# The first chain's spectral product summed on VectorE, with halves exchanged by ScalarE

## The chip, the cores and the metric

The kernel runs on one core of one Trainium2 chip. The metric is the device time of one execution in microseconds (us), and the figure compared is the median of several runs. TensorE (PE in the profile) multiplies matrices, VectorE (DVE) and ScalarE (ACT) work element by element and may read the matmul results in PSUM, GpSimd (POOL) fills tables, and SyncE (SP) issues all the DMAs.

## The reference

Two branches work on the same input `A_u` (2048 positions, 448 channels) and are mixed by a gate:

```python
dt = jnp.exp(log_dt)
A = -jnp.exp(log_A_real) + 1j * A_imag
C = (C_real + 1j * C_imag) * dt[:, None]
P = jnp.exp((A * dt[:, None])[:, :, None] * pos[None, None, :])
K = 2.0 * jnp.einsum("dn,dnl->dl", C, P).real        # 448 kernels, 2048 long, from 256 states each
Kf = jnp.fft.rfft(K, 2 * L)
Uf = jnp.fft.rfft(u_t, 2 * L)
a = irfft(Uf * Kf)[:, :, :L] + u * D_skip            # causal convolution of every channel
b = (sigmoid(x @ w_gate) * (x @ w_up)) @ w_down      # 448 -> 1792 -> 448
g = sigmoid((x * gate_w).sum(-1, keepdims=True))
out = g * a + (1 - g) * b
```

Everything is float32. The change concerns the product `Uf * Kf` and the first step of the inverse transform.

## The kernel before

**Stages.** A prologue makes the parameters. Then `kgen` generates the 448 convolution kernels in 28 chunks of 16 channels, with work on all five engines. The GLU branch (`glu_up`, `glu_down`) is a long stream of matmuls (`gu` for the two projections up, `dn` for the one down) with few demands on other engines. The convolution is a class `Chain`. It makes the spectrum of `u` for both halves of the channels, and later runs once for each half, 224 channels each. The chain of half 0 (called chain 0 here) has its data in the tile `fx_fu`, its PSUM in `fps_fups` (two buffers) and the spectrum of `u` in `uax_fk`. The chain of half 1 (chain 1) has `fx_fk`, `fps_fkps` (three buffers) and `ua_fk`. Both chains run late, side by side, with GLU matmuls between them.

**One chain.** The long transform is split into two short ones with a transpose between. `stage1` multiplies by the first table (L812) and ScalarE copies the results back (L815). `transpose` goes through DRAM for chain 0 (four DMAs to `shf`, four back) and over VectorE for chain 1 (eight `STREAM_TRANSPOSE`, L826). Then `product` walks over eight blocks of four rows. In each block `spectrum_four` (L845) makes two PSUM tiles `p[0]` and `p[1]`, of 128 partitions by 448, by four matmuls on 64 by 64 quadrants of the array; `product_four` multiplies and transforms back (L889); ScalarE copies the two results to `x` (L762). At the end the data are transposed back, and `back` multiplies by the last table (L926), and VectorE scales by the gate and adds to the GLU's part (L930).

**The product.** A spectrum is complex. In a PSUM tile the real parts stand in one group of 32 partitions and the imaginary parts in the next. DRAM holds the spectrum of `u` in a form in which the real part (c = 0) and the imaginary part (c = 1) are each repeated over both groups, so `ua` has the shape 128 x 2 x 2 x 448: partition, c, z, columns. VectorE multiplies both c at once by the same `p[z]` (L879, 896 columns). The sum of the complex product is then left to TensorE. The constant `m_sb` holds the inverse matrix and a second one, turned by a quarter (multiplied by i); the matmuls for c = 0 use the first and those for c = 1 the second, and both accumulate in the same PSUM tile `y[z]`. That makes eight matmuls for a block.

**The order of the work** is not found by a run-time scheduler. The kernel records every operation with its engine, cost, operands and priority (`op`), and the table `PLACE` gives for every kind (engine, tile, priority) the places that its operations take in their engine's queue. `Plan.order` merges the five queues by a small clock model, and the instructions are issued in that order. Each engine works its queue strictly in order. Semaphores are then set between the engines by what each instruction reads and writes.

Tags name the buffers of a pool. `SX` and `SK` give their numbers for the two chains: `ft` tables, `ua` tiles of `u`'s spectrum, `fps` PSUM tiles.

Of the kernel before, what the change touches and what calls it, by code (L numbers as in the profile page):

```python
# [28 lines left out]
    ('Act', 'aci', 10): (15, 36,),  # L29
    ('Act', 'aci', 19): (64, 87,),  # L30
    ('Act', 'acr', 10): (13, 34, 43,),
    ('Act', 'acr', 19): (60, 85, 94,),
# [26 lines left out]
    ('Act', 'dots', 1): (27,),  # L59
    ('Act', 'dots', 2): (50,),  # L60
    ('Act', 'dots', 16): (80, 82,),
# [18 lines left out]
    ('Act', 'idn', 10): (14,),  # L80
    ('Act', 'junk', 10): (28, 61,),
    ('Act', 'junk', 19): (73, 83, 117,),
# [12 lines left out]
    ('Act', 'pos_sb', 10): (75, 53,),  # L95
# [607 lines left out]
def gated_mix(ctx: ExitStack, tc, u, ut, aim, cre, cim, ldt, dskip, gw,  # L703
# [60 lines left out]
    class Chain:  # L764
# [111 lines left out]
        def product_four(self, ua, b):  # L876
# [15 lines left out]
            for z in range(2):  # L892
                evac(lambda r=2 * b + z: self.pair(r), y[z], [(x, 2 * b + z)], prio)
# [685 lines left out]
```

## Time and profile before

| | |
|---|---|
| median of 3 runs | 691.63 us (690.64 to 692.07) |
| the profiled execution's own time | 690.16 us |
| its span, from first to last instruction | 688.4 us |
| instructions | 16283 |
| DMA | 123.84 MB, 180 GB/s on average |
| mean granted TensorE clock | 0.999 |

The profile is one execution. Its span is 1.76 us shorter than the time of the same execution, for what lies before the first and behind the last instruction, and that time lies 1.47 us under the median of the runs. A group row gives line, engine, operation, `out<-in` with tile names, the shape, the count, and then busy time, mean ns of one, and the engine's idle time just before with what ended it. A timeline row begins with its start and its length, and `x8` at its end merges eight instructions. In a table of windows each engine has its busy time and, in brackets, its number of instructions. A float32 matmul appears as two records.

### The profile page before, as it was taken

What the parts mean: (1) busy time and instruction counts of PE and PEld (TensorE: products, weight loads), DVE (VectorE), ACT (ScalarE), POOL (GpSimd) and SP (SyncE); (2) the same over time, 40 slices, a digit from 0 to 9 for tenths busy, and PEclk for the clock granted to TensorE, in tenths of its full rate; (3) what the DMA queues carried; (4) which work ended last, traced back from release to release, by engine and by line L of the source; (5) the groups of instructions that cost most, each with busy time, mean ns of one, the idle gap of its engine ahead of it and who ended that gap; (6) DMA issues with size and microseconds to landing.
All of it is one profiled execution on the core that took longest, in us unless ns stands there. A gap on an engine that the chain in (4) does not pass through costs nothing.

```text
span 688.4 us, 16283 instructions
## 1 busy us (share of the span) xinstructions
PE 673.8 (98%) x6588; PEld 483.1 (70%) x6588; DVE 602.0 (87%) x699; ACT 510.0 (74%) x928; POOL 274.9 (40%) x280
## 2 busy tenths in 40 slices
PE   9999999999999999999899999999999999999996
PEld 8776667877886687775556676788888766556873
DVE  5999999999999999989999789999973489577976
ACT  5677699899999999999999999999941352233110
POOL 0315268865447656675663845667000000000000
PEclk9999999999999999999999999999999999999999
DMA  9769342656896787737966974457948973979866
GB/s 252 180 177 246 87 108 70 153 138 237 186 182 157 177 215 178 225 112 177 193 171 144 233 199 90 140 168 184 180 100 202 271 235 124 312 246 241 166 179 165
DMA packets 97474, 123.84 MB, mean 180 GB/s; under 512 B 31096, under 2 KB 80568, under 8 KB 96376
## 3 DMA queue, kind: packets, MB, share of 16 engines
q1 hardware_dynamic: 97400, 122.81, 69.8%
q8 instruction: 52, 0.85, 0.5%
q14 instruction: 22, 0.18, 0.1%
HBM read 79.20 MB, written 43.58 MB: 178 GB/s over the span
## 4 chain that ended last, share of the span: by engine, by line
PE 73%; ACT 10%; DVE 8%; DMA 5%; issue 2%; SPq 1%; ACTq 0%; DVEq 0%
PE gu_gps L1414 9%; PE gu_gps L1415 8%; PE gu_gps L1416 8%; PE kp_egp L1281 6%; PE dn_gps L1433 5%; PE dn_gps L1435 4%; PE tp_egp L1232 4%; PE dn_gps L1436 4%; PE dn_gps L1437 4%; PE tp_egp L1223 4%; PE fps_fups L812 3%; PE gu_gps L1418 3%; PE gu_gps L1419 3%; PE fps_fups L845 2%; PE fps_fups L889 2%
## 5 line engine op out<-in xcount | busy, mean ns | idle before, releaser
L1414 PE MATMUL gu_gps<-xs_glu,wh_glu 128*128 128x512 f32 x336 | 144.5, 430 | 1.4 <-DVE hl_glu L1400 0.9
L1416 PE MATMUL gu_gps<-xs_glu,wl_glu 128*128 128x512 f32 x336 | 131.8, 392 | 0.0
L1415 PE MATMUL gu_gps<-xs_glu,wh_glu 128*128 128x512 f32 x336 | 131.7, 392 | 0.0
L1269 DVE TENSOR_TENSOR cs_eg<-cs_eg,es_eg 128x2048 f32<-128x2048 f32 x56 | 129.2, 2307 | 1.4
L1252 DVE TENSOR_TENSOR es_eg<-tb_eg 128x1024 f32<-128x1024 f32 x112 | 110.5, 1003 | 3.0 <-POOL tb_eg L1216 0.9
L1213 POOL TENSOR_TENSOR tb_eg<-tb_eg 128x96 f32<-128x96 f32 (+2 forms) x84 | 107.5, 1284 | 5.9
L1216 POOL TENSOR_TENSOR tb_eg<-tb_eg,bs_eg 128x32 f32<-128x32 f32 x84 | 83.9, 1001 | 5.8
L1414 PEld LDWEIGHTS gu_gps<-xs_glu,wh_glu 128*128 128x128 f32 x336 | 63.2, 188 | 30.2 <-issue 13.0
L1398 ACT ACTIVATE sg_glu<-gu_gps 128x512 f32<-128x512 f32 x56 | 33.7, 603 | 58.3 <-PE gu_gps L1419 58.3
L1266 DVE TENSOR_TENSOR cs_eg<-cs_eg,es_eg 128x1024 f32<-128x1024 f32 x56 | 70.5, 1260 | 7.2 <-ACT cs_eg L1245 6.0
L1229 ACT ACTIVATE nn_eg<-cs_eg 128x512 fp32r<-128x512 f32 x112 | 71.7, 640 | 4.5 <-PE tp_egp L1232 2.9
L1415 PEld LDWEIGHTS gu_gps<-xs_glu,wh_glu 128*128 128x128 f32 x336 | 63.3, 188 | 15.4 <-issue 4.8
L1416 PEld LDWEIGHTS gu_gps<-xs_glu,wl_glu 128*128 128x128 f32 x336 | 63.1, 188 | 14.5
L1452 DVE SCALAR_TENSOR_TENSOR ob_glu<-dn_gps,og,ob_glu 128x448 f32<-128x448 f32 x72 | 48.7, 676 | 25.1 <-PE dn_gps L1437 24.1
L1234 ACT ACTIVATE cs_eg<-tp_egp 128x512 f32<-128x512 f32 x112 | 66.5, 605 | 4.1 <-PE tp_egp L1232 3.6
L1227 ACT ACTIVATE cs_eg<-tp_egp 128x512 f32<-128x512 f32 x112 | 67.9, 607 | 1.6 <-PE kp_egp L1281 0.6
L1235 ACT ACTIVATE cs_eg<-tp_egp 128x512 f32<-128x512 f32 x112 | 67.3, 606 | 1.6 <-PE tp_egp L1232 1.4
L1245 ACT ACTIVATE cs_eg<-cs_eg,half_pi 128x1024 f32<-128x1024 f32 x56 | 65.2, 1165 | 0.4
L1281 PEld LDWEIGHTS kp_egp<-cs_eg 128*32 128x32 f32 x3584 | 51.5, 110 | 11.7 <-issue 6.3
L1281 PE MATMUL kp_egp<-cs_eg 128*32 128x64 f32 x3584 | 56.3, 220 | 0.5 <-issue 0.4
L1203 POOL MEMSET tb_eg<- 128x96 f32 x28 | 7.8, 285 | 116.4 <-DVE es_eg L1252 105.5
L1232 PE MATMUL tp_egp<-nn_eg,idn 128*128 128x512 f32 x112 | 49.7, 444 | 3.9 <-ACT nn_eg L1229 3.4
(161 smaller groups left out, 1326.2 us busy)
## 6 DMA issues: line engine op xcount, KB each, us to landing
shf<-fx_fu SPq DMA_DIRECT2D x16, 896.0 KB
fx_fu<-shf SPq DMA_DIRECT2D x16, 896.0 KB
us<-fx_fu SPq DMA_DIRECT2D x16, 896.0 KB
xr_glu<-in_w_dram SPq DMA_DIRECT2D x46, 256.0 KB
uax_fk<-us SPq DMA_DIRECT2D x16, 448.0 KB
ua_fk<-us SPq DMA_DIRECT2D x16, 448.0 KB
xr_glu<-in_w_dram SPq DMA_DIRECT2D x17, 224.0 KB
gt_pre<-in_u_dram SPq DMA_DIRECT2D x8, 448.0 KB
```

The source lines that it names most:

```text
L1213: pool(96 * m, lambda n=n, m=m: G.tensor_mul(g3(n + 1, m), g3(1, m), g3(n, 1).to_broadcast([128, 32, 3, m])))
L1216: pool(32, lambda e=e: G.tensor_mul(t(e + 1), t(e), b(3)))
L1227: op("Act", c_act(512, True), lambda: S.activation(cs[:, 1, ds, 32:96], block(tp), AF.Copy, bias=MAGIC), [tp], [(cs, ("s", i))], prio)
L1229: op("Act", c_act(512), lambda: S.activation(block(nn), cs[:, 1, ds, 32:96], AF.Copy, scale=-1.0, bias=MAGIC), [(cs, ("s", i))], [nn], prio)
L1232: op("PE", c_mm(532), lambda: T.matmul(tp.real, idn.real, nn.real, start=False, stop=True, skip_group_check=True), [nn, idn], [tp], prio)
L1252: V.tensor_mul(o.rearrange("p d (i k) -> p d i k", k=ny), x.unsqueeze(3).to_broadcast([128, 16, nx, ny]), y.unsqueeze(2).to_broadcast([128 ...
L1266: op("DVE", c_dve(1024), lambda: V.tensor_mul(cs[:, :, :, 0:32], cs[:, ::-1, :, 63:31:-1], es[:, :, 0:32].unsqueeze(1).to_broadcast([128, ...
L1269: op("DVE", c_dve(2048), lambda: V.tensor_mul(cs[:, :, :, 32:96], cs[:, :, :, 32:96], es[:, :, 32:96].unsqueeze(1).to_broadcast([128, 2, 1 ...
L1281: T.matmul(kp[32 * j:32 * j + 32, q], cs[:, z, 4 * j + q, 64:96], cs[:, z, 4 * j + q, 0:64], start=cs is parts[0] and z == 0 and q == 0, s ...
L1414: T.matmul(p.real, wh[:, k, cs], x[:, k], start=(k == 0), stop=False)
L1415: T.matmul(p.real, wh[:, k, cs], x[:, 4 + k], start=False, stop=False)
L1416: T.matmul(p.real, wl[:, k, cs], x[:, k], start=False, stop=False)
```

## The change

For half 0 alone (`SWAP = (0,)`), the two terms of the complex product are summed ahead of the inverse matmul. The real part of `u`'s spectrum is multiplied by `p[z]` as before, in place and for 448 columns instead of 896. For the imaginary part, ScalarE copies `p[z]` into a new tile `sw` in four pieces of 32 partitions; each piece is read from the neighbouring group, and the pieces that become real parts change their sign. VectorE multiplies `sw` by the imaginary part and adds the result to the first product. The inverse then needs the plain matrix only: four matmuls a block instead of eight. Half 1 is as before. `PLACE` is a new table throughout, since the new operations need places and the others were moved with them.

```diff
-SX = {'ft': 1, 'ua': 2, 'fps': 2}
-SK = {'ft': 2, 'ua': 2, 'fps': 3}
+SX = {'ft': 1, 'ua': 2, 'fps': 2, 'sw': 2}
+SK = {'ft': 2, 'ua': 2, 'fps': 3, 'sw': 2}
+SWAP = (0,)
+PIECE = 540.0
 ...
         def product_four(self, ua, b):
             x, prio, p = self.x, self.prio, self.spectrum_four(b)
+            if self.h in SWAP:
+                self.product_swapped(ua, b, p)
+                return
 ...
+        def product_swapped(self, ua, b, p):
+            prio = self.prio
+            for z in range(2):
+                sw = self.tile("sw", (128, D))
+
+                def turn(z=z, sw=sw):
+                    for a in range(4):
+                        S.activation(sw[32 * a:32 * a + 32], p[z][32 * (a ^ 1):32 * (a ^ 1) + 32, :D], AF.Copy,
+                                     scale=1.0 if a % 2 else -1.0)
+                op("Act", 4 * PIECE, turn, [p[z]], [sw], prio)
+                op("DVE", c_dve(D, False), lambda z=z: V.tensor_mul(ua[:, 0, z], ua[:, 0, z], p[z][:, :D]),
+                   [p[z]], [(ua, (0, z))], prio)
+                op("DVE", c_dve(D), lambda z=z, sw=sw: V.tensor_mul(sw.real, ua[:, 1, z], sw.real),
+                   [(ua, (1, z))], [sw], prio)
+                op("DVE", c_dve(D), lambda z=z, sw=sw: V.tensor_add(ua[:, 0, z], ua[:, 0, z], sw.real),
+                   [sw], [(ua, (0, z))], prio)
+            y = [self.psum(1), self.psum(1)]
+
+            def f():
+                for z in range(2):
+                    for i in range(2):
+                        rows, to = slice(64 * i, 64 * i + 64), slice(64 * (i ^ z), 64 * (i ^ z) + 64)
+                        T.matmul(y[z][to, :D], m_sb[rows, 64:128], ua[rows, 0, z], start=True, stop=True)
+            op("PE", c_mm64(D), f, [(ua, (0, 0)), (ua, (0, 1)), m_sb], y, prio)
+            for z in range(2):
+                evac(lambda r=2 * b + z: self.pair(r), y[z], [(self.x, 2 * b + z)], prio)
 ...
-    ('Act', 'fx', 40): (669, 681, 687, 691, 699, 704, 714, 718, 733, 735, 742, 745, 748, 749, 754, 758, 844, 839, 858,
+    ('Act', 'fx', 40): (670, 686, 694, 700, 705, 708, 720, 721, 726, 729, 741, 743, 747, 749, 763, 768, 843, 842, 860,
+    ('Act', 'swx', 40): (824, 826, 847, 854, 862, 864, 872, 873, 880, 881, 888, 890, 896, 897, 905, 906,),
```

The order in which the built programs stand shows three places. The lines of the changed kernel are those of its own source there: L831 is the old L826, L850 the old L845, L887 the old L879, L897 the old L889, L1438 the old L1403, L1487 the old L1452. L910 is the turned copy on ScalarE, L913 the product with `p[z]`, L915 that with `sw`, L917 the sum, L925 the new inverse. A number behind a tile's name is that of the buffer's use.

First place: VectorE while chain 1 is transposed for the first time (`fx_fk`, eight transposes). Before, from the first transpose on:

```order
L826 STREAM_TRANSPOSE fx_fk_6546<-fx_fk_6546 128x28x32 x3
L1403 SCALAR_TENSOR_TENSOR sg_glu_6882<-sg_glu_6882,gu_gps_6861 128x512
L826 STREAM_TRANSPOSE fx_fk_6546<-fx_fk_6546 128x28x32 x3
L1403 SCALAR_TENSOR_TENSOR sg_glu_6932<-sg_glu_6932,gu_gps_6919 128x512
L826 STREAM_TRANSPOSE fx_fk_6546<-fx_fk_6546 128x28x32
L1452 SCALAR_TENSOR_TENSOR ob_glu_5499<-dn_gps_6762,og,ob_glu_5499 128x448
```

And in the changed kernel, from the second transpose on:

```order
L831 STREAM_TRANSPOSE fx_fk_6541<-fx_fk_6541 128x28x32
L913 TENSOR_TENSOR uax_fk_6784<-uax_fk_6784,fps_fups_6885 128x448
L831 STREAM_TRANSPOSE fx_fk_6541<-fx_fk_6541 128x28x32
L913 TENSOR_TENSOR uax_fk_6784<-uax_fk_6784,fps_fups_6884 128x448
L831 STREAM_TRANSPOSE fx_fk_6541<-fx_fk_6541 128x28x32
L1438 SCALAR_TENSOR_TENSOR sg_glu_6938<-sg_glu_6938,gu_gps_6895 128x512
L915 TENSOR_TENSOR swx_fk_6917<-uax_fk_6784,swx_fk_6917 128x448
L831 STREAM_TRANSPOSE fx_fk_6541<-fx_fk_6541 128x28x32
L915 TENSOR_TENSOR swx_fk_6899<-uax_fk_6784,swx_fk_6899 128x448
L831 STREAM_TRANSPOSE fx_fk_6541<-fx_fk_6541 128x28x32
```

The six VectorE instructions of chain 0's third block now lie between the transposes. Before, the two 896-column products of a block lay there, ahead of the last transpose.

Second place: TensorE in the middle of the product, where both chains run. Before, the inverses of the two chains with chain 1's ahead, and then chain 1's next spectrum:

```order
L889 MATMUL fps_fkps_7121<-ua_fk_7045,m_sb 64x448 x2
L889 MATMUL fps_fkps_7122<-ua_fk_7045,m_sb 64x448 x2
L889 MATMUL fps_fkps_7121<-ua_fk_7045,m_sb 64x448 x2
L889 MATMUL fps_fkps_7122<-ua_fk_7045,m_sb 64x448 x2
L889 MATMUL fps_fups_7134<-uax_fk_7005,m_sb 64x448 x2
L889 MATMUL fps_fups_7135<-uax_fk_7005,m_sb 64x448 x2
L889 MATMUL fps_fups_7134<-uax_fk_7005,m_sb 64x448 x2
L889 MATMUL fps_fups_7135<-uax_fk_7005,m_sb 64x448 x2
L845 MATMUL fps_fkps_7149<-fx_fk_6546,m_sb 64x448 x2
L845 MATMUL fps_fkps_7150<-fx_fk_6546,m_sb 64x448 x2
```

In the changed kernel, at chain 0's fourth block:

```order
L925 MATMUL fps_fups_7099<-uax_fk_6877,m_sb 64x448 x2
L925 MATMUL fps_fups_7100<-uax_fk_6877,m_sb 64x448 x2
L897 MATMUL fps_fkps_7107<-ua_fk_6879,m_sb 64x448 x2
L897 MATMUL fps_fkps_7108<-ua_fk_6879,m_sb 64x448 x2
L897 MATMUL fps_fkps_7107<-ua_fk_6879,m_sb 64x448 x2
L897 MATMUL fps_fkps_7108<-ua_fk_6879,m_sb 64x448 x2
L850 MATMUL fps_fups_7122<-fx_fu_5114,m_sb 64x448 x2
L850 MATMUL fps_fups_7123<-fx_fu_5114,m_sb 64x448 x2
```

Chain 0's inverse has half its rows and stands directly ahead of chain 1's, which needs the product that VectorE makes from `fps_fkps_7082` and `fps_fkps_7083`.

Third place: VectorE for the same block, with the semaphores that a row waits for in brackets (`Activation` is ScalarE's, `DMAHW` a DMA queue's):

```order
L913 TENSOR_TENSOR uax_fk_6877<-uax_fk_6877,fps_fups_7026 128x448 [waits DMAHW1_49,PE_49,Activation_49]
L915 TENSOR_TENSOR swx_fk_7037<-uax_fk_6877,swx_fk_7037 128x448 [waits DMAHW0_49]
L913 TENSOR_TENSOR uax_fk_6877<-uax_fk_6877,fps_fups_7025 128x448
L1487 SCALAR_TENSOR_TENSOR ob_glu_4705<-dn_gps_6931,og,ob_glu_4705 128x448 [waits PE_49]
L915 TENSOR_TENSOR swx_fk_7057<-uax_fk_6877,swx_fk_7057 128x448 [waits DVE_49]
L917 TENSOR_TENSOR uax_fk_6877<-uax_fk_6877,swx_fk_7037 128x448 [waits DVE_49]
L917 TENSOR_TENSOR uax_fk_6877<-uax_fk_6877,swx_fk_7057 128x448 [waits DVE_49]
L887 TENSOR_TENSOR ua_fk_6879<-ua_fk_6879,fps_fkps_7083 128x2x448 [waits DMAHW5_49,DMAHW2_49,PE_49]
L887 TENSOR_TENSOR ua_fk_6879<-ua_fk_6879,fps_fkps_7082 128x2x448
```

The first row reads `p[1]` and writes over a part of `uax`, and it waits for ScalarE although it uses nothing that ScalarE made: ScalarE's turned copy reads the same PSUM tile, and the two readers of one PSUM tile are kept apart, whichever was issued first. The row for `swx_fk_7057`, which does use the copy, then needs no wait on ScalarE of its own. Before, a block of chain 0 had two rows in all here, of 896 columns each, and none waited for ScalarE.

More of the change, by code (lines that the diff above doesn't have):

```diff
@@ L28 @@
 PLACE = {
[L29 to L32, printed above, removed]
[26 rows of a table removed]
-    ('Act', 'dots', 1): (27,),
-    ('Act', 'dots', 2): (50,),
-    ('Act', 'dots', 16): (80, 82,),
[18 rows of a table removed]
-    ('Act', 'idn', 10): (14,),
-    ('Act', 'junk', 10): (28, 61,),
-    ('Act', 'junk', 19): (73, 83, 117,),
[12 rows of a table removed]
-    ('Act', 'pos_sb', 10): (75, 53,),
[22 rows of a table removed]
-    ('DVE', 'aci', 10): (44,),
+    ('Act', 'aci', 10): (14, 38,),
+    ('Act', 'aci', 19): (61, 87,),
+    ('Act', 'acr', 10): (12, 35, 48,),
+    ('Act', 'acr', 19): (63, 84, 96,),
[26 rows of a table added]
+    ('Act', 'dots', 1): (26,),
+    ('Act', 'dots', 2): (51,),
+    ('Act', 'dots', 16): (77, 82,),
[18 rows of a table added]
+    ('Act', 'idn', 10): (15,),
+    ('Act', 'junk', 10): (28, 58,),
+    ('Act', 'junk', 19): (76, 79, 114,),
[12 rows of a table added]
+    ('Act', 'pos_sb', 10): (75, 74,),
[6 rows of a table added]
+    ('Act', 'swx', 40): (824, 826, 847, 854, 862, 864, 872, 873, 880, 881, 888, 890, 896, 897, 905, 906,),
[16 rows of a table added]
+    ('DVE', 'aci', 10): (47,),
     ('DVE', 'aci', 19): (109,),
-    ('DVE', 'acr', 10): (85,),
+    ('DVE', 'acr', 10): (82,),
     ('DVE', 'acr', 19): (148,),
[1 row of a table removed]
[1 row of a table added]
     ('DVE', 'ai', 19): (145,),
[2 rows of a table removed]
[2 rows of a table added]
     ('DVE', 'ci', 10): (67,),
[10 rows of a table removed]
-    ('DVE', 'dtp', 10): (39,),
-    ('DVE', 'dtv', 10): (29,),
[14 rows of a table removed]
-    ('DVE', 'half_pi', 0): (1,),
[24 rows of a table removed]
-    ('DVE', 'ones', 10): (0,),
-    ('DVE', 'p', 10): (15, 16, 17, 18, 20, 21, 24,),
-    ('DVE', 'phs', 20): (105,),
[6 rows of a table removed]
-    ('DVE', 'skip', 20): (27,),
[6 rows of a table removed]
-    ('DVE', 'uax', 40): (538, 537, 545, 544, 561, 560, 569, 570, 573, 576, 581, 582, 586, 587, 592, 593, 622, 623,
[10 rows of a table removed]
[10 rows of a table added]
+    ('DVE', 'dtp', 10): (43,),
+    ('DVE', 'dtv', 10): (30,),
[14 rows of a table added]
+    ('DVE', 'half_pi', 0): (22,),
[24 rows of a table added]
+    ('DVE', 'ones', 10): (2,),
+    ('DVE', 'p', 10): (16, 17, 18, 19, 20, 28, 29,),
+    ('DVE', 'phs', 20): (1,),
[6 rows of a table added]
+    ('DVE', 'skip', 20): (0,),
+    ('DVE', 'swx', 40): (534, 535, 547, 553, 566, 564, 580, 583, 592, 594, 603, 606, 613, 616, 625, 627,),
[6 rows of a table added]
+    ('DVE', 'uax', 40): (536, 540, 533, 538, 543, 550, 545, 554, 561, 571, 559, 568, 581, 584, 579, 585, 589, 595,
[11 rows of a table added]
     ('DVE', 'x', 10): (10,),
     ('DVE', 'xr', 10): (9,),
[14 rows of a table removed]
[14 rows of a table added]
         1032, 1035, 1038, 1041, 1042,),
     ('PE', 'fps', -1): (0,),
[43 rows of a table removed]
[43 rows of a table added]
     ('Pool', 'bsx1', 10): (5, 11,),
```

507 rows, old and new, of the table PLACE are left out of this document.

## The prediction

> **What bounds the kernel now.** The page first: busy time by engine, then the 40 slices of 17.2 us.
>
> ```profile
> PE 673.8 (98%) x6588; PEld 483.1 (70%) x6588; DVE 602.0 (87%) x699; ACT 510.0 (74%) x928; POOL 274.9 (40%) x280
> ...
> PE   9999999999999999999899999999999999999996
> ...
> DVE  5999999999999999989999789999973489577976
> ACT  5677699899999999999999999999941352233110
> ```
>
> TensorE is busy for 98% of the span, and at least nine tenths in nearly every slice. From slice 30 on (516 us), when kernel generation is over, ScalarE is mostly free and VectorE has gaps. There the two chains run, and the change lies there. The table of windows, TensorE first, then weight loads, VectorE, ScalarE:
>
> ```profile
> 540.00:560.00 20.00, 20.00 (x136) 12.69 (x135) 9.48 (x13) 10.59 (x23) 0.00 (x0) 1.00 0.87 262
> 560.00:580.00 20.00, 20.00 (x105) 14.34 (x106) 19.58 (x17) 5.85 (x11) 0.00 (x0) 1.00 0.46 154
> 580.00:600.00 20.00, 20.00 (x154) 10.38 (x154) 14.55 (x16) 5.56 (x12) 0.00 (x0) 1.00 0.81 269
> 600.00:620.00 20.00, 20.00 (x161) 10.05 (x163) 13.24 (x16) 6.10 (x12) 0.00 (x0) 1.00 0.78 259
> 660.00:688.40 28.40, 22.30 (x146) 14.88 (x144) 18.95 (x40) 1.86 (x3) 0.00 (x0) 0.96 0.67 168
> ```
>
> From 540 to 620 us TensorE never pauses: a microsecond taken from it is a microsecond of the whole, as long as nothing else is late in its place. VectorE is full from 560 to 580 (the transposes of chain 1), and then has 12 us free of 40. The order is fixed, so a late VectorE result stops TensorE and everything queued behind it.
>
> **The change, term by term.** Times of one piece of work:
>
> ```profile
> 577.44 1.66 PE fps_fups L889 x16
> ...
> 585.54 1.50 PE fps_fups L889 x16
> ...
> 630.17 0.43 PE gu_gps L1414
> ...
> 630.83 0.23 PE gu_gps L1416
> ...
> 632.43 0.20 PE dn_gps L1435
> ```
>
> These are pieces of the chain that ended last. An inverse of eight matmuls (16 records) takes 1.50 us behind other work on 64 by 64 quadrants and 1.66 behind full-size matmuls, and the first full-size matmul behind such work takes 0.43 instead of 0.23: a visit to the small shape costs 0.16 + 0.20 = 0.36 beside its work.
>
> *Term 1, removed.* Each of chain 0's eight blocks loses half an inverse, 0.75 us: **-6.0 us** of TensorE. The changed order has 178 stretches of one shape where there were 176, a visit more: **+0.4**.
>
> *Added beside it.* VectorE and ScalarE:
>
> ```profile
> 583.11 2.08 DVE L879 TENSOR_TENSOR uax_fk<-uax_fk,fps_fups 128x896 f32<-128x896 f32 x2
> ...
> 620.78 0.68 DVE L1406 TENSOR_TENSOR hl_glu<-sg_glu,hh_glu 128x512 fp32r<-128x512 f32 x1
> 621.38 0.68 DVE L1381 TENSOR_TENSOR wl_glu<-xr_glu,wh_glu 128x512 fp32r<-128x512 f32 x1
> ```
>
> Two products of 896 columns take 2.08, so one begins 1.00 after the other (the next begins 0.08 ahead of an end). At 512 columns that step is 0.60 (620.78 to 621.38). In between, 448 columns make 0.54. A block had 2.0 us of VectorE and now has six such steps, 3.2.
>
> ```profile
> 621.49 0.98 ACT L762 ACTIVATE fx_fu<-fps_fups 128x448 f32<-128x448 f32 x2 [4.92 <-PE fps_fups L889]
> ...
> L815 ACT ACTIVATE fx_fk<-fps_fkps 128x448 f32<-128x448 f32 x16 | 8.1, 544 | 11.2 <-PE fps_fkps L812 11.2
> ...
> L1347 DVE TENSOR_TENSOR xs_glu<-xr_pre,xs_glu 128x256 fp32r<-128x256 f32 x4 | 1.7, 423 | 0.1
> L1348 DVE TENSOR_TENSOR xs_glu<-xr_pre,xs_glu 64x256 fp32r<-64x256 f32 x4 | 1.7, 422 | 0.1
> ```
>
> No ScalarE copy of 32 partitions is in the trace. On VectorE half the partitions take the same time (423 and 422 ns), so I take the copy of 128 partitions: two in 0.98, a step of 0.44; four pieces 1.86 us, eight 3.6. The bounds are this and 0.54 a piece without overlap (L815's mean). Even at 0.54 the 64 pieces are 35 us of an engine that is busy for under 30 of the 80 us above; as a sum they are hidden. What counts is the **delay in a block**: before, spectrum, two products, inverse; now eight copies and a longer queue. I follow the order as built, shown above. "GLU" is full-size work at 0.23 (gu) and 0.20 (dn).
>
> *Term 2, the transposes of chain 1.*
>
> ```profile
> 557.23 1.03 PE L812 MATMUL fps_fkps<-fx_fk,ft_fk 64*128 64x224 f32 x8
> ...
> 578.92 0.95 PE L845 MATMUL fps_fkps<-fx_fk,m_sb 64*64 64x448 f32 x8
> ...
> 559.30 5.55 DVE L826 STREAM_TRANSPOSE fx_fk<-fx_fk 128x896 f32<-128x896 f32 x3
> ...
> 576.95 1.90 DVE L826 STREAM_TRANSPOSE fx_fk<-fx_fk 128x896 f32<-128x896 f32 x1
> ```
>
> Chain 1's first spectrum needs all eight transposes. Before, 20.7 us of TensorE work lay between the last stage-1 matmul (558.2) and this spectrum (578.92), and the last transpose ended at 578.85: it fitted to 0.1 us. Now TensorE has there 64 gu, 9 dn, three half visits of 0.75 and three changes of shape: 14.7 + 1.8 + 2.25 + 1.1 = 19.9. VectorE has eight transposes at 1.84 (5.55 for three), six steps of 0.54 of chain 0's block and three others of 0.60: 14.7 + 3.2 + 1.8 = 19.7, and starts some 1.2 behind the stage (559.30 - 558.2 = 1.1 before). TensorE waits 20.9 + 0.1 - 19.9: **+1.2**.
>
> *Term 3, the fourth block* (the second and third places shown). Count from the end of its spectrum. ScalarE's eight copies end at 3.3 (they begin when the first half is ready, 0.37 before). The first VectorE row waits for them. Seven steps and two times 0.1 for results used at once bring the last sum to 7.3. TensorE comes to the inverse at 6.65 (9 dn, 8 gu, an inverse, a spectrum, 0.7 for shapes), waits for both sums and ends 0.3 late, at 7.7. Right behind stands chain 1's inverse, whose two products were queued behind those sums: 7.3 + 2.08 = 9.4. Another 1.7: **+2.0**.
>
> *Term 4, the fifth block.* VectorE's first row waits for the first four copies (1.6), and chain 1's two products behind it end at 4.2, while TensorE is at their inverse at 3.2; its first quarter runs, the rest waits: 0.8. The remaining five rows end at 7.0 and TensorE needs them at 6.5: 0.4. **+1.2**. The last three blocks have 6 us and more of GLU and chain 1 in the gap: **+0.3** for all.
>
> A rule of the Trainium skill speaks against this change here. "PSUM — Partial Sum Buffer", section "PSUM bank collisions raise a hardware error", says that two engines may not be in the same PSUM bank and partitions at once, and counts ScalarE reading beside VectorE reading. The old kernel never reads a tile from both, so its trace says nothing on it. By the rule the first of a block's products stands behind the copies, as the waits in the built order have it; without it terms 3 and 4 would shrink to some 1.6 together, and the sum would be about 1.6 lower.
>
> *Term 5, chain 0's way through DRAM.*
>
> ```profile
> 648.00:650.00 2.00, 2.00 (x11) 1.70 (x10) 1.92 (x3) 0.00 (x0) 0.00 (x0) 1.00 0.98 319
> 650.00:652.00 2.00, 2.00 (x16) 1.38 (x16) 2.00 (x2) 0.00 (x0) 0.00 (x0) 1.00 0.04 13
> ...
> 651.13 0.60 PE L926 MATMUL fps_fups<-fx_fu,ftx_fk 128*64 128x224 f32 x4
> ```
>
> The last result is copied by 622.47 (above); the DMA share falls from 0.98 to 0.04 at 650, so the way takes 27.5 us, and `back` began 1.1 behind. Now 69 gu, 45 dn, chain 1's inverse and three of its `back` groups fill 28.3 from the inverse on, 27.3 from its copy. **+0.3**.
>
> **Sum**: -6.0 + 0.4 + 1.2 + 2.0 + 1.2 + 0.3 + 0.3 = -0.6. On the profiled 690.16 that is 689.6; its runs' median lies 1.47 above, so **691.0** against 691.63. Before the stage the two orders nearly agree: at the last kernel chunk both have issued 924 gu and 216 dn rows, and I put no difference there. Bounds: at VectorE's least (0.5 a step) and with planned waits alone (1.1 in term 3, 0.4 in term 2), -4.1 us or 687.5; with 0.6 a step, 0.54 a piece and waits in the last blocks too, +3, or 694.6.
>
> **Rivals.**
> *The saving is kept.* For it: VectorE waited for chain 0's spectra, so it had room:
>
> ```profile
> L879 DVE TENSOR_TENSOR uax_fk<-uax_fk,fps_fups 128x896 f32<-128x896 f32 x16 | 16.7, 1081 | 9.9 <-PE fps_fups L845 9.5 <-DMA xr_glu<-in_w_dram 0.5
> ```
>
> 9.9 us of idle against 10 more of work. Against it: the room lies where TensorE's order no longer waits. If half of terms 2 to 5 comes to nothing, -3.1: 688.5.
> *Slower: the copies hold the chain.* If a piece takes 0.54 or more, eight take 4.3, the fourth and fifth blocks end 0.7 later each, and the last three, whose gaps I found full to within 0.5, fall behind too: 5 x 0.7 = 3.5, or 694.5. It decides from a step of about 0.5. For it: a cross-group copy is unknown; against it: the 0.44 of every other PSUM copy here.
> *TensorE does not get its 6 us.* If a half inverse does not take half, the waits stay and the gain goes: 695. L889's even steps speak against it.
>
> **Chances.** Forecast (689.7 to 692.3) 0.45; saving kept 0.30; copies slow 0.20; TensorE unchanged 0.05. A run of this kernel can tell about 0.2% (1.4 us, 690.25 to 693.0) from no change. The forecast gives 0.08 to faster and 0.36 to same; the first rival 0.28 to faster; of the others 0.23 is slower. Faster 0.36, same 0.39, slower 0.25. Range 687.5 to 694.5.
>
> **What will show it.** L925 at 0.75 to 0.91 us a block (eight records each, 64 in all). TensorE waiting on L831 ahead of chain 1's first spectrum (1.2), and on L917 and L887 in two blocks (3.2). A step of 0.44 on L910. VectorE rows of L913 that wait for L910. `back` on `fx_fu` waiting for DMA by under 1 us. TensorE's busy time 5 to 6 us less, its idle time 5 more. I am wrong if TensorE stays without waits from 540 to 625, or if L910's step is above 0.5.

## The result: slower by 1.3%, and the profile after

| | before | after |
|---|---|---|
| median of the runs on one chip | 691.85 us (690.64 to 692.78, 4 runs) | 701.50 us (700.78 to 702.52, 4 runs) |
| profiled execution, its span | 690.16 us, 688.4 us | 701.74 us, 699.6 us |
| mean granted TensorE clock | 0.999 | 0.991 |

The ratio is 1.0134, with a 95% interval of 1.0104 to 1.0165. The forecast was 691.0 and its range ended at 694.5, so the prediction was wrong. The spans of the two profiled executions, which the rest explains, differ by 699.6 - 688.4 = 11.2 us.

The page of the changed kernel, busy time by engine and slices (now of 17.5 us):

```profile
PE 677.0 (97%) x6524; PEld 483.3 (69%) x6524; DVE 611.6 (87%) x731; ACT 544.6 (78%) x992; POOL 266.3 (38%) x280
...
PE   8999999999997999998999999999999999899996
...
DVE  5999999999995999999998899899962698679976
ACT  5677798899996999999999999999933674675110
```

TensorE has 64 instructions fewer, as meant. Yet its busy time did not fall by 6 us, it rose by 3.2, from 673.8 to 677.0. And there is a dip in slice 12 (from 210 us on), far ahead of the product, on all three engines at once. Before had none there. The list of waits shows what it is (engine, line and tile that wait, what ended the wait: us in total, times, longest):

```profile
PE gu_gps L1449 <- DVE sg_glu L1438: 5.0, 1, 5.0
PE tp_egp L1267 <- ACT nn_eg L1264: 2.9, 5, 1.8
...
PE dn_gps L1470 <- DVE ob_glu L1487: 1.6, 2, 0.8
PE dn_gps L1468 <- DVE ob_glu L1487: 1.1, 2, 0.8
PE fps_fkps L897 <- issue: 1.1, 1, 1.1
...
PE fps_fkps L897 <- DVE ua_fk L887: 0.9, 1, 0.9
...
PE fps_fkps L850 <- DVE fx_fk L831: 0.2, 1, 0.2
...
PE fps_fups L925 <- DVE uax_fk L917: 0.2, 1, 0.2
```

The same list of before, whose longest wait is 1.1 us:

```profile
PE tp_egp L1232 <- ACT nn_eg L1229: 3.4, 7, 0.9
PE fps_fups L1030 <- DVE half_pi L1497: 1.1, 1, 1.1
```

**The early wait.** A single wait of 5.0 us on a GLU matmul. VectorE around it, in the timeline (start, duration, engine, line, operation), and then TensorE:

```profile
210.29 0.67 DVE L1487 SCALAR_TENSOR_TENSOR ob_glu<-dn_gps,og,ob_glu 128x448 f32<-128x448 f32 x1
210.89 2.36 DVE L1304 TENSOR_TENSOR cs_eg<-cs_eg,es_eg 128x2048 f32<-128x2048 f32 x1
213.28 1.23 DVE L1287 TENSOR_TENSOR es_eg<-tb_eg 128x1024 f32<-128x1024 f32 x1
214.43 0.75 DVE L1416 TENSOR_TENSOR wl_glu<-xr_glu,wh_glu 128x512 fp32r<-128x512 f32 x1
215.10 0.67 DVE L1438 SCALAR_TENSOR_TENSOR sg_glu<-sg_glu,gu_gps 128x512 f32<-128x512 f32 x1
```

```profile
210.33 0.49 PE L1267 MATMUL tp_egp<-nn_eg,idn 128*128 128x512 f32 x1 [0.17 <-ACT nn_eg L1264]
215.83 0.80 PE L1449 MATMUL gu_gps<-xs_glu,wh_glu 128*128 128x512 f32 x1 [5.00 <-DVE sg_glu L1438]
```

The matmul starts a new PSUM tile, and it waits until VectorE has read the tile that lay in that buffer. The order of the built program names the tiles (engine, the operation's place in that engine's queue, the row):

```
TensorE  726 L1449 MATMUL gu_gps41_2524<-xs_glu1_227,wh_glu9_1470 128x512 [waits DVE_49]
VectorE  269 L1438 SCALAR_TENSOR_TENSOR sg_glu19_2239<-sg_glu19_2239,gu_gps39_2222 128x512
ScalarE  287 L1433 ACTIVATE sg_glu19_2239<-gu_gps38_2195 128x512 [waits PE_49]
ScalarE  314 L1433 ACTIVATE sg_glu20_2502<-gu_gps40_2337 128x512 [waits DVE_49]
```

There are two buffers for these tiles. Tile 40 was read by ScalarE at 208.50 to 209.13, 1.7 us before TensorE came to tile 41 at 210.83, so its buffer was free. But in the built program tile 41 got the buffer of tile 39, which VectorE read last in its row, until 215.77. The clock model that merges the queues lets a new tile take whichever buffer is free first, and so saw no wait there.

The wait did not come alone. The table of windows (span, TensorE, weight loads, VectorE, ScalarE, GpSimd, then the granted clock):

```profile
210.00:212.00 2.00, 0.65 (x2) 0.19 (x1) 2.00 (x3) 2.00 (x6) 2.00 (x2) 1.00 0.10 19
212.00:214.00 2.00, 0.00 (x0) 0.00 (x0) 1.97 (x2) 0.64 (x2) 1.92 (x2) 0.76 0.12 38
214.00:216.00 2.00, 0.17 (x1) 0.18 (x2) 2.00 (x4) 0.00 (x0) 1.49 (x3) 0.50 0.00 0
216.00:218.00 2.00, 2.00 (x7) 0.96 (x11) 0.98 (x2) 0.00 (x0) 0.88 (x3) 0.50 0.47 131
218.00:220.00 2.00, 2.00 (x11) 0.84 (x4) 0.00 (x0) 0.76 (x2) 1.76 (x4) 0.53 0.00 0
```

From 213.0 to 219.9 the clock is half (0.24 x 2 us x 2 = 0.96 us of the second window, all of the next two, 1.88 us of the last). TensorE works at half speed for the 4.1 us after 215.83 and loses 2.0 more. That stretch also shows why busy time rose: the matmul at 215.83 counts 0.80 us, where rows of its kind at full clock take 0.39.

**The product stage.** From 540 to 620 TensorE never paused before. Now:

```profile
560.00:580.00 20.00, 19.31 (x97) 13.59 (x94) 18.83 (x20) 14.09 (x27) 0.00 (x0) 1.00 0.69 241
580.00:600.00 20.00, 17.93 (x117) 9.63 (x118) 16.26 (x22) 9.30 (x18) 0.00 (x0) 1.00 0.42 141
600.00:620.00 20.00, 18.77 (x129) 8.82 (x127) 14.63 (x21) 13.71 (x27) 0.00 (x0) 1.00 0.73 244
```

4.0 us of pauses. The fourth block in the timeline, ScalarE and VectorE and then TensorE:

```profile
587.41 4.39 ACT L910 ACTIVATE swx_fk<-fps_fups 32x448 f32<-32x448 f32 x8 [0.48 <-PE fps_fups L850]
591.82 0.54 ACT L767 ACTIVATE fx_fk<-fps_fkps 128x448 f32<-128x448 f32 x1
...
591.83 0.62 DVE L913 TENSOR_TENSOR uax_fk<-uax_fk,fps_fups 128x448 f32<-128x448 f32 x1 [2.02 <-ACT swx_fk L910]
...
593.43 0.68 DVE L1487 SCALAR_TENSOR_TENSOR ob_glu<-dn_gps,og,ob_glu 128x448 f32<-128x448 f32 x1
...
595.63 2.08 DVE L887 TENSOR_TENSOR ua_fk<-ua_fk,fps_fkps 128x896 f32<-128x896 f32 x2
```

```profile
589.94 1.73 PE L897 MATMUL fps_fkps<-ua_fk,m_sb 64*64 64x448 f32 x16
591.50 1.89 PE L850 MATMUL fps_fkps<-fx_fk,m_sb 64*64 64x448 f32 x8
...
594.17 0.47 PE L1470 MATMUL dn_gps<-vh_glu,hh_glu 128*128 128x448 f32 x1 [0.78 <-DVE ob_glu L1487]
...
595.67 1.07 PE L925 MATMUL fps_fups<-uax_fk,m_sb 64*64 64x448 f32 x8
597.81 1.74 PE L897 MATMUL fps_fkps<-ua_fk,m_sb 64*64 64x448 f32 x16 [1.07 <-issue]
```

Eight copies take 4.39 us, 0.55 each. VectorE's first product waits 2.02 for them, and everything behind it on VectorE is late, the GLU row L1487 included. The wait of 1.07 listed under "issue" belongs here too: that inverse reads what L887's second product wrote, and this ended 0.10 us before, at 597.71. Look at the spectrum at 591.50: eight records take 1.89 us. Before, the same eight (L845) took 0.93 to 1.08 in a visit, and so do most of them now. Its second PSUM tile can only start when ScalarE's copy at 591.82 has emptied a buffer, and that copy stands behind the eight. **No wait is listed for it.** In the 64 by 64 shape records overlap (each takes about 0.55 us, and in the inverse at 589.94 four begin within 0.02 us and the next four 0.43 later); if a part of a visit is late, the rows ahead of it fill the gap on paper, and no idle time is left to list.

So I measured the loss without the wait lists: from the time of a point of TensorE's program I take away the work issued up to it, rows of each kind times their step when they run back to back (0.227 us a gu row, 0.199 a dn row, 0.0945 a row of 64 by 64, the other kinds likewise). What is left is time without work, changes of shape and half clock included. For the start of the last kernel chunk, the first `back` (chain 0's before, chain 1's in the new orders), and the end:

| profiled execution | last kernel chunk | first `back` | end | product stage (second less first) |
|---|---|---|---|---|
| before | 74.8 | 84.4 | 94.3 | 9.6 |
| after | 82.7 | 102.9 | 111.6 | 20.2 |

The change costs 7.9 us early and 10.6 in the product stage; the tail gives back 1.2; the 64 rows removed are 64 x 0.0945 = 6.05. 7.9 + 10.6 - 1.2 - 6.05 = 11.2, the difference of the spans. Within the stage, the 15 visits to the 64 by 64 shape, each counted to the start of the next full-size row, took 2.8 us more than their rows before and 10.7 after: 7.9 of the 10.6, of which the wait lists show only 2.6 (1.6 inside the visits, 1.0 at their ends). The two other waits of the stage make 1.6, and 1.1 is left, most of it at the dn rows, which now stand in 38 stretches where before had 33.

### The profile page after: what moved, and what is told of

Its sections match the earlier page's. It is cut to its first block, busy times and chain, and to the rows that moved or that the text cites. A ratio compares the mean times of both kernels' runs of the same rounds, so it can differ in the third digit from the quotient of the medians.

```text
span 699.6 us, 16225 instructions
## 1 busy us (share of the span) xinstructions
PE 677.0 (97%) x6524; PEld 483.3 (69%) x6524; DVE 611.6 (87%) x731; ACT 544.6 (78%) x992; POOL 266.3 (38%) x280
## 4 chain that ended last, share of the span: by engine, by line
PE 80%; ACT 11%; DVE 6%; issue 2%; ACTq 0%; DVEq 0%
PE gu_gps L1449 10%; PE gu_gps L1451 9%; PE gu_gps L1450 9%; PE dn_gps L1468 9%; PE kp_egp L1316 6%; PE dn_gps L1470 4%; PE tp_egp L1267 4%; PE tp_egp L1258 4%; PE gu_gps L1453 3%; PE dn_gps L1471 3%; PE dn_gps L1472 3%; PE gu_gps L1454 3%; PE fps_fups L817 3%; PE fps_fups L850 2%; DVE fx_fk L831 2%
## 5 line engine op out<-in xcount | busy, mean ns | idle before, releaser
L1287 DVE TENSOR_TENSOR es_eg<-tb_eg 128x1024 f32<-128x1024 f32 x112 | 112.9, 1030 | 2.1
L1248 POOL TENSOR_TENSOR tb_eg<-tb_eg 128x96 f32<-128x96 f32 (+2 forms) x84 | 110.1, 1314 | 5.9
L1251 POOL TENSOR_TENSOR tb_eg<-tb_eg,bs_eg 128x32 f32<-128x32 f32 x84 | 69.5, 830 | 5.8
L1487 DVE SCALAR_TENSOR_TENSOR ob_glu<-dn_gps,og,ob_glu 128x448 f32<-128x448 f32 x72 | 48.7, 676 | 13.9 <-PE dn_gps L1472 12.8
L1316 PEld LDWEIGHTS kp_egp<-cs_eg 128*32 128x32 f32 x3584 | 51.3, 110 | 10.7 <-issue 7.2
L1470 PE MATMUL dn_gps<-vh_glu,hh_glu 128*128 128x448 f32 x136 | 53.4, 392 | 1.7 <-DVE ob_glu L1487 1.6
```

The costliest lines, as they stand in the source:

```text
L1248: pool(96 * m, lambda n=n, m=m: G.tensor_mul(g3(n + 1, m), g3(1, m), g3(n, 1).to_broadcast([128, 32, 3, m])))
L1251: pool(32, lambda e=e: G.tensor_mul(t(e + 1), t(e), b(3)))
L1287: V.tensor_mul(o.rearrange("p d (i k) -> p d i k", k=ny), x.unsqueeze(3).to_broadcast([128, 16, nx, ny]), y.unsqueeze(2).to_broadcast([128 ...
L1316: T.matmul(kp[32 * j:32 * j + 32, q], cs[:, z, 4 * j + q, 64:96], cs[:, z, 4 * j + q, 0:64], start=cs is parts[0] and z == 0 and q == 0, s ...
L1470: T.matmul(p[:, :D], hh[:, ts], vh.real, start=(i == 0), stop=False)
```

## The experiments

The theory was: the early loss is one misplaced VectorE row, and the stage's loss comes from ScalarE and VectorE reading one PSUM tile in turn. The rivals: the early loss lies spread over the re-made table; and the stage's loss comes from the added work as such, or from the new order whatever its operations cost. The early repair is a part of all kernels below except before_gu_late and after_again; early_old and new_order get it by other tables. "Before" is the kernel before on the same chip; the single runs scatter more in these batches (689.1 to 696.3 for before) than in the first.

**gu_moved** takes VectorE's read of tile 39 five rows earlier; nothing else changes but the numbers between.

```diff
-    ('DVE', 'sg', 21): (230, 237, 248, 269, 275, 287,),
+    ('DVE', 'sg', 21): (230, 237, 248, 264, 275, 287,),
```

> The changed kernel with one VectorE row moved: the product of a GLU tile (L1438) that TensorE waited 5.0 us for at 210 us stands four rows earlier. Theory A (one tile that waits for the buffer of a late reader, and the half clock behind that wait, made the early 7 us): TensorE has no wait at that place and no clock of 0.5 behind it, and the time falls by about 7, from 701.5 to 694.4 (693.5 to 695.5). Rival B (the loss lies in the new operations of the product stage): within 1 us of 701.5. Rival C (the low clock has another cause than the wait): only the 5.0 us go, 696.5.

Measured: median 698.57 (694.42 to 702.40, 9 runs), before 692.41, ratio 1.0074 (1.0041 to 1.0107). The profiled run is the fastest, 694.42, as theory A has it. The 5.0 us wait has gone from its list, no stretch ahead of the tail runs at half clock, and the time without work at the last kernel chunk is 74.3, where before has 74.8. In this run the whole early loss has gone with one row. The stage still costs 20.7. The median misses what was expected: it lies 4 us above that run, only 2.9 under the changed kernel's 701.50. What may stand behind this is told at the end.

**gu_fk_moved** also takes a ScalarE copy of chain 1 in the fifth block ahead of that block's turned copies, since a PSUM buffer of chain 1 was given back behind them.

```diff
-        882, 883, 886, 889, 891, 900, 895, 904, 901, 908, 907, 916, 915,),
+        880, 883, 886, 889, 891, 900, 895, 904, 901, 908, 907, 916, 915,),
...
-    ('Act', 'swx', 40): (824, 826, 847, 854, 862, 864, 872, 873, 880, 881, 888, 890, 896, 897, 905, 906,),
+    ('Act', 'swx', 40): (824, 826, 847, 854, 862, 864, 872, 873, 881, 882, 888, 890, 896, 897, 905, 906,),
```

> As before, and one ScalarE copy of chain 1 (L767, the one that frees the buffer for which chain 1's third inverse waits) put ahead of the eight turned copies of chain 0's fifth block. Theory A: the wait of 1.1 us ahead of L897 at 596 us goes, and with it what queued behind it, some 3 us: 691.0 (690.5 to 692.5). Rival B (the turned copies themselves hold the chain, and are now 0.4 us later): no further gain, 694.4 or more.

Measured: 695.93 (694.68 to 698.03, 12 runs), ratio 1.0059 (1.0038 to 1.0079). The stage went from 20.7 to 20.2 only. That this one buffer carried the stage's loss is refuted. (The median is 2.6 lower than that of gu_moved, but the intervals of the two ratios overlap.)

**before_gu_late** puts the same fault into the kernel before: a VectorE row of the same kind goes behind the three that followed it.

```diff
-    ('DVE', 'sg', 21): (226, 239, 246, 264, 276, 282,),
+    ('DVE', 'sg', 21): (226, 239, 249, 264, 276, 282,),
```

> The kernel before the change with one VectorE row moved: a GLU product (L1403) behind three rows of kernel generation, so that TensorE finds its buffer 4.0 us late. Theory A (a long wait of TensorE costs itself and is followed by a stretch at half clock): 691.9 + 4.0 + 1.7 to 3.4 = 697.6 to 699.3, a clock of 0.5 for one or two stretches of 3.4 us. Rival C (the wait costs itself and no more): 695.9.

Measured: 697.41 (694.48 to 704.40, 9 runs), ratio 1.0077 (1.0043 to 1.0110). Its list of waits now begins with

```profile
PE gu_gps L1414 <- DVE sg_glu L1403: 4.1, 1, 4.1
```

and the 6.8 us from 192.8 on run at half clock, where TensorE, back at 194.4, loses 2.6. The time without work at the last kernel chunk is 84.3 against 74.8. Of these 9.5 us, 4.1 + 2.6 are the fault's; the rest lies in waits elsewhere that the profile of before doesn't have, 1.1 for a load at 28 us and 1.6 under "issue" at 488. The median, 5.0 above before, is just under what theory A expected. The product code of before is untouched here, so the fault costs time by itself.

**one_copy** (on top of gu_fk_moved) makes one whole copy in place of the four turned pieces.

```diff
-                    for a in range(4):
-                        S.activation(sw[32 * a:32 * a + 32], p[z][32 * (a ^ 1):32 * (a ^ 1) + 32, :D], AF.Copy,
-                                     scale=1.0 if a % 2 else -1.0)
+                    S.activation(sw.real, p[z][:, :D], AF.Copy)
```

> As gu_fk_moved, but ScalarE copies each spectrum tile once, all 128 partitions in place, instead of in four turned pieces (so the halves are not exchanged and the signs not changed). Eight copies a block (4.4 us) become two (0.9 us). Theory A (the order as built hides the copies): within 1 us of gu_fk_moved. Rival B (the copies, and VectorE's first product that waits behind them, hold the chain): 3 to 6 us less than gu_fk_moved.

Measured: 692.87 (689.37 to 694.84, 12 runs), ratio 1.0003 (0.9981 to 1.0025). The stage falls from 20.2 to 16.1. The wait of VectorE's product on the copies is all but gone (0.4, where gu_fk_moved had 6.3), though the two engines still take turns at the tile.

**after_again and gu_again** are the changed kernel and gu_moved once more, beside the kernels of the second batch.

> The changed kernel once more, unchanged, beside its one-row variant on the same chip (the first four variants ran on a chip whose runs spread by 7 us). All theories: about 9.7 above before, with the wait of 5.0 us ahead of L1449 and 6.8 us of clock 0.5 behind it in every profile.

> The changed kernel with the one VectorE row moved up, once more. Theory A (the early 7.4 us are one late buffer and the clock behind it): 7 less than the changed kernel, 2.5 to 4.5 above before. Rival B (the first comparison was a matter of the chip): less than 5 between the two.

Measured: after_again 700.82 (699.57 to 701.41, 5 runs), ratio 1.0126 (1.0101 to 1.0151); gu_again 697.95 (693.79 to 699.68, 9 runs), ratio 1.0078 (1.0052 to 1.0103), with before at 691.91. The stage's 20.1 and 20.6 repeat the first profiles to 0.1. But the two medians differ by 2.9 as in the first batch, not by the 7 that theory A expected, and the profile of gu_again has lost 80.0 by the last kernel chunk: the wait of 5.0 is gone and another stop has come, which the end of this document shows.

**no_share** (on top of gu_fk_moved) keeps all copies and all VectorE rows, but the product L913 multiplies by a column of an SBUF tile, so VectorE no longer reads the PSUM tile that ScalarE copies.

```diff
-                op("DVE", c_dve(D, False), lambda z=z: V.tensor_mul(ua[:, 0, z], ua[:, 0, z], p[z][:, :D]),
-                   [p[z]], [(ua, (0, z))], prio)
+                op("DVE", c_dve(D, False), lambda z=z: V.tensor_mul(ua[:, 0, z], ua[:, 0, z], m_sb[:, 0:1].to_broadcast([128, D])),
+                   [m_sb], [(ua, (0, z))], prio)
```

> As gu_fk_moved, but VectorE's first product of a swapped block (L913) multiplies by a column of a constant instead of the spectrum tile in PSUM, which leaves the spectrum out of the real part. ScalarE still makes its eight turned copies of 0.55 us. Theory D (what the copies cost comes by way of VectorE, which may not read a tile beside ScalarE and waits behind four or eight copies): the 3.9 us between gu_fk_moved and one_copy go, in the product stage 14.8 us without work instead of 18.7. Theory E (it comes by way of ScalarE itself, whose small copies of the other chain stand behind the eight): under 1 us gained.

Measured: 693.50 (687.98 to 695.68, 12 runs), ratio 1.0017 (0.9994 to 1.0039). The groups of ScalarE's copy and of this product, whose last field is the idle time ahead and what ended it, first as changed and then here:

```profile
L910 ACT ACTIVATE swx_fk<-fps_fups 32x448 f32<-32x448 f32 x64 | 34.3, 536 | 4.8 <-DVE uax_fk L913 2.5 <-PE fps_fups L850 1.0 <-issue 0.3
...
L913 DVE TENSOR_TENSOR uax_fk<-uax_fk,fps_fups 128x448 f32<-128x448 f32 x16 | 9.6, 611 | 11.8 <-ACT swx_fk L910 8.5 <-PE fps_fups L850 3.3
```

```profile
L910 ACT ACTIVATE swx_fk<-fps_fups 32x448 f32<-32x448 f32 x64 | 34.3, 536 | 2.1 <-PE fps_fups L850 0.8 <-issue 0.3 <-ACT fx_fk L767 0.2
...
L913 DVE TENSOR_TENSOR uax_fk<-uax_fk,m_sb 128x448 f32<-128x448 f32 x16 | 9.7, 618 | 0.0
```

Same counts and durations of work, no wait, and the stage falls from 20.2 to 15.2: that VectorE reads the tile which ScalarE copies costs **5.0 us**. This is an upper bound for the taking of turns, since L913 no longer waits for the spectrum itself either ("PE fps_fups L850" in the row). one_copy, which keeps that wait and has short copies, gained 4.1. The ratios to before differ by 0.42 points, or 2.9 us, less than the stage gained; early, this profile has 3.2 more than gu_fk_moved. The excess in the 64 by 64 visits falls from 11.8 to 6.7 with it, so what looked like long matmul records there were waits.

**small_ops** (on top of one_copy) lets the product with the copy and the sum run on 8 columns only.

```diff
-                op("DVE", c_dve(D), lambda z=z, sw=sw: V.tensor_mul(sw.real, ua[:, 1, z], sw.real),
+                op("DVE", c_dve(D), lambda z=z, sw=sw: V.tensor_mul(sw[:, :8], ua[:, 1, z, :8], sw[:, :8]),
...
-                op("DVE", c_dve(D), lambda z=z, sw=sw: V.tensor_add(ua[:, 0, z], ua[:, 0, z], sw.real),
+                op("DVE", c_dve(D), lambda z=z, sw=sw: V.tensor_add(ua[:, 0, z, :8], ua[:, 0, z, :8], sw[:, :8]),
```

> As one_copy, and VectorE's product with sw and its sum take 8 columns instead of 448, so that the swapped half of the product is left out. VectorE loses 32 x 0.45 = 14 us of work, ScalarE has two short copies a block: nearly nothing of the new operations is left, only their places in the order. Theory F (the 6 us that remain in one_copy lie in where the new order puts the old work): within 1 us of one_copy. Rival G (they are VectorE's longer way through a block): 3 to 6 us less than one_copy, and less than before.

Measured: 692.30 (688.03 to 694.40, 12 runs), ratio 1.0001 (0.9981 to 1.0021). The stage is 14.7: VectorE's longer work is worth only 1.4. And 14.7 is still 5.1 above before although little of the added work is left. By elimination, a third part would sit in the new places of the old rows.

**early_old** has the old table's places up to the last kernel chunk and the changed ones behind it; **new_order** has the whole computation of the changed kernel, with a table of my own that gives the stage other places, under the condition that no tile gets a buffer that comes free later than the clock model says. Both tables differ in hundreds of numbers.

> The old table's order for everything up to the last kernel chunk (505 us) and the changed kernel's order from there on; the operations are those of the changed kernel. If the early loss belongs to the new table alone and the product stage loses its 10.6 us whatever stands ahead: before + 10.6 - 6.05 - 1.2 (the shorter tail) = before + 3.4, 695.3 (694.5 to 696.5), with TensorE's time without work within 0.5 us of before up to the last chunk and no stall at 210 or 240 us. Rival: the product stage suits its new prefix badly or well, and the difference moves by over 2 us either way.

> The same operations and the old order up to the last chunk, and from there an order of my own: ScalarE's eight copies and VectorE's first products are placed so that neither stands ahead of a row for which TensorE waits, and no tile takes the buffer of a late reader. Theory D+F (the product stage lost its time to the readers of one PSUM tile that wait for each other and to the places of old rows): most of the 10.6 us go and the saved 6.05 us come out, 689 to 692, at or below before. Rival G (the longer way of a block costs this much in any order): 694 or more.

Measured, with before at 691.21: early_old 696.32 (694.04 to 699.99, 6 runs), ratio 1.0080 (1.0051 to 1.0108); new_order 692.66 (689.32 to 696.08, 12 runs), ratio 1.0016 (0.9999 to 1.0032). In early_old 75.7 us without work at the last kernel chunk and 20.4 in the stage: the early part is repaired by other means than in gu_moved, and the stage keeps its loss to 0.2 us. In new_order the stage takes 16.1 with every operation of the change in it, 1.5 of it a wait for one load of chain 1. So 4.3 us of the stage were only the order. They can't be added to the 5.0 of no_share, since the new operations have other places too: VectorE's L913 waits 2.3 us for the copies here, where early_old has 8.5. How much is due to the old rows alone was not separated. The profiled run is the slowest of the twelve; its 79.8 early come mostly from a stop of 2.9 us under "issue" at 479 us with half clock behind it. By its median new_order is as fast as before, within 0.3%, and not faster. No version that computes everything beat the kernel before.

All stages side by side, in the profiled executions:

| | last kernel chunk | product stage | what it has |
|---|---|---|---|
| before | 74.8 | 9.6 | |
| after, after_again | 82.7, 81.6 | 20.2, 20.1 | |
| gu_moved, gu_again | 74.3, 80.0 | 20.7, 20.6 | early row moved |
| gu_fk_moved | 78.1 | 20.2 | and one copy moved |
| one_copy | 79.3 | 16.1 | and one copy for four |
| no_share | 81.3 | 15.2 | gu_fk_moved, PSUM tile not shared |
| small_ops | 79.2 | 14.7 | one_copy, products small |
| early_old | 75.7 | 20.4 | old places early |
| new_order | 79.8 | 16.1 | other places in the stage |
| before_gu_late | 84.3 | 9.6 | before, early row late |

## Why the prediction was wrong, step by step

*"Before the stage the two orders nearly agree … I put no difference there."* This step failed first, and for 7.9 us, more than the 7.0 by which the result lies above the range. I had counted rows at the last kernel chunk. That says how much has been issued by then, not what it waited for on the way. gu_moved and before_gu_late show the cause, by taking it out and by putting it in: one VectorE row that is five places too late for the buffer that its tile frees, 5.0 us of waiting and 2.0 of half clock. early_old, with the old table up to there, has no such loss (75.7). A second stretch of half clock (at the end of this document) is another 1.7; it stands behind another wait, and no run ties it to the row. Together that is 8.7; where 0.8 of it came back is not resolved. In the medians the repair brought only 2.9.

*Terms 2 to 5*, 5.0 us for the stage and 5.4 with the extra visit, measured 10.6. The mechanism of terms 3 and 4 was right: VectorE's L913 waits for ScalarE's copies (8.5 us in all), its tail delays chain 1's inverse, and TensorE waits. Their size was wrong, and the runs show two places where, which overlap.
- The step of a copy is 0.55, not 0.44, and lies above even my upper bound of 0.54. I had named 0.5 as the point from which the rival "the copies hold the chain" decides, and that rival was the one that came true. It was priced at 3.5 us over the forecast; no_share puts all of the shared tile at 5.0, of which the forecast had a part. No run changed the step of a copy alone. The rule of the Trainium skill ("PSUM — Partial Sum Buffer", "PSUM bank collisions raise a hardware error"), that ScalarE and VectorE may not read the same bank and partitions at once, is what the built program follows: its waits keep the two apart, at the price of up to those 5.0 us. No run here lets both read at once.
- I counted planned waits at the ends of blocks, and took the places of the old rows as harmless. small_ops leaves 5.1 us there with little added work, and new_order gets 4.3 back by places alone, those of the new rows included. Most of it is inside the 64 by 64 visits (small_ops: 6.1 us of excess, before 2.8), where no list of waits has it.

*Term 2 by itself* was too dear. Of 1.2 us ahead of chain 1's first spectrum the list shows 0.2, and the visit around it took 2.95 us, where one of 24 rows took 2.41 before: 0.5 in all.

*Term 1* was right. The 64 rows removed are worth 6.05 us, and a half inverse takes 0.98 to 1.07 with the change of shape inside. The visit more did not come in this stage, which has 15 before and after. *Term 5* (0.3) came to nothing: no wait on a DMA at `back` in the list, and the tail gave back 1.2.

Of the signs I gave, two misled. "TensorE's busy time 5 to 6 us less" came out as 3.2 more, since half clock and hidden waits stretch the records. "L917 and L887 in two blocks (3.2)" came as 0.2 and 0.9, with 1.1 under "issue" and 0.8 on L1487, and the rest without a name. And the rival "the saving is kept" was never near: even small_ops, which drops most of the cost, only reaches the time of before. One sign held: "I am wrong … if L910's step is above 0.5".

## What to carry to other kernels

A change that comes with a regenerated table of places is two changes. Compare the waits of the bound engine in every stage, and which buffer each new tile gets, not only the rows that the diff speaks of: one row five places later cost 7.0 us here, in waiting and half clock, more than the whole gain of 6.05.
Where two engines read one PSUM tile, put the first one's full time into the chain of the second, and take the step of a copy from a row of its own shape; if there is none, the forecast's range has to hold the rival.
Measure the loss of TensorE as time minus rows times step. Lists of waits leave out what is lost inside groups of small matmuls that overlap, here 5.3 of 10.6 us.

## What the runs showed of the hardware that was not expected

**Half clock comes in stretches of 3.41 us.** After the 5.0 us wait there were two (6.83 us), as after the 4.1 of before_gu_late. A wait of 1.79 us up to 317.69 in the changed kernel was followed by one (the clock is the third number from the end):

```profile
318.00:322.00 4.00, 3.95 (x13) 1.85 (x12) 3.17 (x4) 3.93 (x8) 0.00 (x0) 0.61 0.79 156
```

while the same wait in gu_moved, 1.78 us up to 310.66, was followed by none:

```profile
310.00:314.00 4.00, 3.14 (x13) 1.54 (x13) 3.92 (x5) 3.94 (x9) 0.00 (x0) 1.00 0.88 183
314.00:318.00 4.00, 3.44 (x15) 2.03 (x16) 4.00 (x6) 3.74 (x8) 1.62 (x3) 1.00 0.81 147
```

"TensorE: Matmul & The Clock Gate" of the Trainium skill, "Part 1: The HAM clock gate", tells of a free-running window of about 3.4 us after whose idleness the clock is halved. The stretches agree with its length. But a wait of 1.8 us, half a window, was enough in both profiles of the changed kernel (after_again has it too), and was not in the six of gu_moved, gu_again, gu_fk_moved, one_copy, no_share and small_ops, where it is as long. What decides was not tested.

**A stop of TensorE beside a fetch of instructions.** In gu_again it stands still for 3 us with nothing to release it:

```profile
239.36 0.40 PE L1258 MATMUL tp_egp<-pos_sb,phs 97*128 97x512 f32 x1
242.71 0.37 PE L1470 MATMUL dn_gps<-vh_glu,hh_glu 128*128 128x448 f32 x1 [2.95 <-issue]
```

The DMA queue "q8 instruction" has 51 packets in an execution, 16 KB each. One of them runs from 240.54 to 241.50, and TensorE goes on 1.2 us after it. At that time the DMA engines are full (share 1.05 from 240 to 241), with stores of 896 KB of `u`'s spectrum under way. gu_fk_moved, one_copy, no_share and small_ops show the same stop of 2.0 to 3.3 us, which ends each time 1.2 to 1.5 us after such a packet, and a stretch of half clock behind it, which makes some 4.7 us in gu_again. The profiled run of gu_moved has 0.8 there, and full clock, with the DMA engines as full: it is 4.2 and 3.5 us faster than the medians of gu_moved and gu_again. The stops in new_order (2.9, up to 482.09) and before_gu_late (1.6, up to 488.14) end 1.6 and 1.5 us after such a packet, too. The mean clock of the 18 single runs of gu_moved and gu_again fits: the four at 0.998 took 693.8 to 695.4 us, the others, at 0.993 to 0.997, 695.2 to 702.4. This would explain why removing the early wait brought only 2.9 us in the median (700.82 to 697.95), and why these kernels scatter more than the changed one. The link to the fetch rests on the coincidence in eight profiles, and most of the 51 packets are followed by no stop; I did not move the stores to test it.
